# An eighth pair of every block goes through layer two in two fp32r halves, and five pairs carry 1 + ELU

## The chip, the cores and the metric

The kernel runs on one core of a Trainium2 chip. The metric is device time in microseconds (us), the median of several runs of one program. Engines: TensorE (PE, its weight loads PEld), VectorE (DVE), ScalarE (ACT), GpSimd (POOL), and SyncE (SP), which here issues DMAs.

## The reference

An induced-set attention over four batches of 12480 tokens of 128 channels, followed by a feed-forward layer of width 2048 with ELU, all in fp32:

```python
def mab(q, kv):
    s = scale * (q @ kv.transpose(0, 2, 1))
    s = s - s.max(-1, keepdims=True)
    a = np.exp(s)
    a /= a.sum(-1, keepdims=True) + 1e-09
    return a @ kv
h = mab(I, x)          # 32 inducing rows look at x
x = mab(x, h)          # x looks at the 32 rows
...
h = x @ w_in
g = np.where(h > 0.0, h, alpha * (np.exp(np.minimum(h, 0.0)) - 1.0))
return (g @ w_out).astype(np.float32)
```

## The kernel before

A batch is cut into 25 blocks, 15 of 512 tokens and 10 of 480, in seven groups of up to four. For a block the feed-forward runs over eight pairs (`cp` 0 to 7) of 128-wide slices of the hidden layer. The attention of the next batch is done beside the feed-forward of the present one; its operations are four blocks wide and small beside the pairs.

One pair in `unit`: two products of layer one put h + 1 into the PSUM tile `ph` (L980); ScalarE takes e = exp(ph - 1) (L990); VectorE takes g = min(max(ph, 1), e) (L994), which is 1 + ELU(h). What follows depends on the pair's letter:

- P: ScalarE rounds g - 1 to fp32r, `gh` (L1004); GpSimd takes 1 off g (L1020) and then writes the remainder `gl` = (g - 1) - gh (L1024).
- D: g stays in `ph`; ScalarE writes `gh` from it (L1004) and VectorE the remainder `gl` (L1010).
- N: GpSimd takes 1 off g (L1020), and the pair goes into layer two as plain fp32. M is the same with the 1 taken off on ScalarE (L1015).

Layer two (L1060) adds into one PSUM bank `po` of the block. A split pair makes six fp32r products: gh by wo_h, gh by wo_l and gl by wo_h, for two slices. A plain pair makes two fp32 products by `wo_n`. When the eighth pair is in, VectorE transposes `po` into `o` (L1075) and SP sends it off in four DMAs (L1083).

The letters are PDPDPDPN in half of the blocks and PDPDPDPM in the other half; the very first block (z) is plain in all eight pairs and reads the raw weights.

Buffers: three `ph` tiles, two `po` banks (which the small products of the attention also use), 14 rooms `sb` for e, gh and gl, and six homes `stk` that hold the attention weights of a block for layer one, filled by SP's DMAs (L947).

The order of every engine's instructions is worked out before the program is written (`Program.order`). A planner holds each operation with a cost in ns; each engine takes the operation that is ready first, and of several ready ones the one with the lowest key. The key is the number of the pair plus an offset from a table (KP, ATT, FH, KS). The order then stands fixed in the program, and each engine keeps to it.

Of the kernel before, what the change touches and what calls it, by code (L numbers as in the profile page):

```python
# [30 lines left out]
KP = {'g': 52.484375, 'px': 424.125, 'cx': -2637.046875, 'ps': 718.796875, 's': -1844.171875, 'pm': -917.6875, 'bias': -794.59375, 'exp': -1390.671875, 'eT': 883.234375, 'hh': 581.9375, 'h': -1250.90625, 'es': 527.859375, 'end': -196.765625, 'hw': 551.890625, 'win': 621.21875, 'winstep': 254.875, 'wout': -524.234375, 'woutstep': 1444.390625, 'in0': -0.359375, 'in1': 1712.046875, 'out': -245.34375, 'outstep': 241.421875, 'hwlate': 1751.796875, 'lone': -1372.359375}  # L31
# [3 lines left out]
ATT = {'first0': [996.609375, 2382.75, 1612.328125, -78.078125, 1461.875, -1378.578125, -1038.96875, -879.78125, 939.5625, 320.9375, -1571.25, -1430.9375], 'first1': [-671.8125, 1196.203125, -1397.484375, -170.328125, 176.296875, 1510.203125, 1513.703125, -312.28125, -432.71875, 1756.40625, 2562.34375, 4164.34375], 'next0': [-95.265625, -961.65625, 898.078125, 1025.671875, 539.109375, 210.140625, -860.5, 222.375, -1118.4375, -106.53125, -131.3125, 1211.5], 'next1': [-402.421875, -1166.65625, 1288.828125, 287.828125, -181.484375, 1747.34375, 341.53125, 363.625, 414.75, 243.546875, -30.828125, 634.8125], 'rest': [-67.09375, -987.203125, 716.015625, 374.046875, 595.421875, 1159.140625, 1544.3125, 273.578125, 951.0, 1170.5, 1960.46875, 164.15625]}  # L35
FH = {'xq': -451.765625, 'xT': 1142.0625, 'ps': -1349.25, 's': 1938.265625, 'pm': -448.859375, 'bias': -1055.984375, 'xm': 2688.171875, 'exp': 594.0, 'eT': 1467.703125, 'hh': -546.265625, 'h': -836.609375, 'es': 2813.640625, 'r': -1103.875, 'hn': 21.671875, 'hT': -339.75, 'hw': -606.59375}
ROOM = -39.28125
# [4 lines left out]
KINDS = {'a': 'PDPDPDPN', 'l': 'PDPDPDPN', 'z': 'NNNNNNNN', 'b': 'PDPDPDPM', 'm': 'PDPDPDPM'}  # L42
# [278 lines left out]
def kernel(  # L321
# [16 lines left out]
    for n, t in GROUPING:  # L338
# [59 lines left out]
    def new(shape, dtype, tag, name):  # L398
        return prog.tile(pools[tag], shape, dtype, tag, name)
# [20 lines left out]
    nc.gpsimd.memset(largest, 254.0)  # L420
    ind = const.tile([M, C], F32, name="ind")
    indT = const.tile([C, M], F32, name="indT")
    win_sb = const.tile([C, F], F32, name="win_sb")
    wo_n = const.tile([P, max(1, len(CHUNKS_N)), C], F32, name="wo_n")
    wo_m = const.tile([P, max(1, len(CHUNKS_M)), C], F32R, name="wo_m")
# [537 lines left out]
    def unit(b, k, cp):  # L963
# [33 lines left out]
        if how != "N":  # L997
            gh = slot(shape, F32R, f"gh_{n}", 2)
            if how == "V":
                add("DVE", n + K["gh"][cp], 0.66 * 2 * T + 60, lambda: nc.vector.tensor_scalar(  # L1000
                    out=gh(), in0=e(), scalar1=-1.0, scalar2=1.0, op0=ALU.add, op1=ALU.mult
                ), r=[(g, 0)], w=[(gh, 0)], lag=90, lock=True)
            else:
                add("ACT", n + K["gh"][cp], act(2 * T, how == "D")[0] + 20, lambda: nc.scalar.activation(  # L1004
                    gh(), ga(), AF.Copy, bias=-1.0
                ), r=[(g, 0)], w=[(gh, 0)], lag=118)
        if how in "DP":
            gl = slot(shape, F32R, f"gl_{n}", 1)
# [361 lines left out]
```

## Time and profile before

| | us |
|---|---|
| median of 3 runs (lowest, highest) | 1629.22 (1628.21, 1629.85) |
| span of the profiled execution | 1626.7 |
| PE busy | 1617.1 |
| ACT busy | 1523.5 |
| POOL busy | 1518.4 |
| DVE busy | 1487.5 |

Busy time is the union of the records of an engine. A record of a matmul ends after its last column has left the array, so consecutive records overlap; what one matmul costs a saturated TensorE is the distance from its start to the next start. An fp32 product leaves two records.

### The profile page before, as it was taken

Reading aid. Unit: us, or ns where it says so; the run is one execution under the profiler, and the core shown is the slowest. Engines: PE = TensorE matmul, PEld = TensorE weight load, DVE = VectorE, ACT = ScalarE, POOL = GpSimd, SP = SyncE. Lnnn points to the kernel's source line nnn. Section 1 sums busy time; section 2 is a strip of 40 time slices with the busy share of each in tenths; the row PEclk is TensorE's granted clock in tenths of the full one; section 3 lists DMA queues with packets and bytes.
Section 4 is the critical chain, followed back from the end, with each engine's and each line's share of the span. In section 5 each row is a group of like instructions: output and inputs, shape, how many; then the busy total and the mean of one; then the engine's idle time right before and its main releaser. Section 6 shows DMA issues by size and latency. Waiting matters only on the chain.

```text
span 1626.7 us, 23588 instructions
## 1 busy us (share of the span) xinstructions
PE 1617.1 (99%) x7820; PEld 1228.0 (75%) x7820; DVE 1487.5 (91%) x1556; ACT 1523.5 (94%) x1785; POOL 1518.4 (93%) x1018
## 2 busy tenths in 40 slices
PE   9999999999999999999999999999999999999998
PEld 7767777778777777787777777777777777777787
DVE  7799999989999999999999999999989898999997
ACT  8689999999999999999999999999999999999997
POOL 6789999999999999999999999999989999999998
PEclk9999999999999999999999999999999999999999
DMA  7442231423332133332342223322222111112111
GB/s 263 94 81 48 46 79 38 84 50 87 85 69 49 40 59 64 70 57 47 107 86 56 40 47 70 55 59 57 53 52 59 30 24 36 28 33 43 22 19 25
DMA packets 384618, 97.99 MB, mean 60 GB/s; under 512 B 364816, under 2 KB 370736, under 8 KB 384240
## 3 DMA queue, kind: packets, MB, share of 16 engines
q1 hardware_dynamic: 383504, 96.36, 27.8%
q8 instruction: 62, 1.02, 0.3%
q14 instruction: 60, 0.49, 0.1%
q10 hardware_dynamic: 992, 0.12, 0.0%
HBM read 48.94 MB, written 25.56 MB: 46 GB/s over the span
## 4 chain that ended last, share of the span: by engine, by line
PE 93%; ACT 3%; DVE 2%; issue 1%; POOL 0%; DVEq 0%; ACTq 0%; POOLq 0%
PE po L1060 65%; PE ph L980 22%; PE ps_hh L646 2%; ACT e L990 2%; ACT gh L1004 1%; PE ps_ts L803 1%; PE warm L1166 1%; PE ps_ts L558 1%; DVE e L994 1%; PE ps_s L558 1%; PE ps_x L1144 0%; PE ps_t L803 0%; DVE ph L994 0%; PE ps_warm L1109 0%; PE ps_hw L735 0%
## 5 line engine op out<-in xcount | busy, mean ns | idle before, releaser
L1024 POOL TENSOR_TENSOR gl<-e,gh 128x1024 fp32r<-128x1024 f32 (+1 forms) x396 | 931.7, 2358 | 20.0
L990 ACT ACTIVATE e<-ph 128x1024 f32<-128x1024 f32 (+1 forms) x800 | 789.9, 1010 | 58.0 <-PE ph L980 55.4
L994 DVE SCALAR_TENSOR_TENSOR e<-ph,e 128x1024 f32<-128x1024 f32 (+1 forms) x503 | 592.0, 1186 | 69.5 <-ACT e L990 63.0
L1060 PE MATMUL po<-gh,wo_h 128*128 128x512 f32 (+1 forms) x1386 | 542.4, 391 | 0.3 <-ACT gh L1004 0.3
L1060 PE MATMUL po<-gh,wo_l 128*128 128x512 f32 (+1 forms) x1386 | 536.7, 387 | 0.0
L1020 POOL TENSOR_SCALAR e<-e 128x1024 f32<-128x1024 f32 (+1 forms) x452 | 464.5, 1036 | 59.5 <-ACT gh L1004 51.3
L980 PE MATMUL ph<-stk,hw 128*128 128x512 f32 (+1 forms) x1600 | 505.7, 405 | 1.0 <-DVE e L994 0.7
L1004 ACT ACTIVATE gh<-e 128x1024 fp32r<-128x1024 f32 (+1 forms) x396 | 413.2, 1049 | 10.9 <-DVE e L994 10.2
L1060 PE MATMUL po<-gl,wo_h 128*128 128x512 f32 (+1 forms) x1386 | 416.1, 399 | 0.4 <-DVE o L1075 0.3
L994 DVE SCALAR_TENSOR_TENSOR ph<-ph,e 128x1024 f32<-128x1024 f32 (+1 forms) x297 | 354.6, 1194 | 24.1 <-ACT e L990 23.5
L980 PEld LDWEIGHTS ph<-stk,hw 128*128 128x128 f32 x1600 | 295.6, 188 | 98.6 <-issue 30.7
L1010 DVE SCALAR_TENSOR_TENSOR gl<-ph,gh 128x1024 fp32r<-128x1024 f32 (+1 forms) x297 | 351.3, 1184 | 14.9 <-ACT gh L1004 13.5
L1060 PEld LDWEIGHTS po<-gl,wo_h 128*128 128x128 f32 x1386 | 257.3, 188 | 75.2 <-issue 17.2
L1004 ACT ACTIVATE gh<-ph 128x1024 fp32r<-128x1024 f32 (+1 forms) x297 | 300.9, 1015 | 7.8 <-DVE ph L994 6.9
L1060 PEld LDWEIGHTS po<-gh,wo_h 128*128 128x128 f32 x1386 | 260.1, 188 | 60.5 <-ACT gh L1004 6.8
L1060 PEld LDWEIGHTS po<-gh,wo_l 128*128 128x128 f32 x1386 | 260.3, 188 | 53.3 <-issue 3.1
L1060 PE MATMUL po<-e,wo_n 128*128 128x512 f32 (+1 forms) x396 | 181.8, 581 | 0.0
L1060 PEld LDWEIGHTS po<-e,wo_n 128*128 128x128 f32 x396 | 74.4, 189 | 53.3 <-issue 45.4
L1075 DVE STREAM_TRANSPOSE o<-po 128x512 f32<-128x512 f32 (+1 forms) x100 | 69.1, 691 | 5.5 <-PE po L1060 4.9
L1015 ACT ACTIVATE e<-e 128x1024 f32<-128x1024 f32 (+1 forms) x51 | 53.1, 1041 | 0.1
L530 DVE STREAM_TRANSPOSE xT<-xq 128x1024 f32<-128x1024 f32 (+2 forms) x39 | 45.2, 1159 | 0.0
L935 POOL TENSOR_TENSOR alo<-aT,ahi 128x512 fp32r<-128x512 f32 (+3 forms) x28 | 35.8, 1277 | 4.3 <-ACT ahi L933 4.3
(124 smaller groups left out, 645.1 us busy)
## 6 DMA issues: line engine op xcount, KB each, us to landing
xm<-in_x_dram SPq DMA_DIRECT2D x32, 512.0 KB, 4.6
out_dram<-o SPq DMA_DIRECT2D x240, 64.0 KB, 1.9
xq<-in_x_dram SPq DMA_DIRECT2D x84, 128.0 KB, 3.0
out_dram<-o SPq DMA_DIRECT2D x158, 60.0 KB, 1.9
stk<-ahi SPq DMA_DIRECT2D x118, 64.0 KB, 2.0
xq<-in_x_dram SPq DMA_DIRECT2D x60, 120.0 KB, 2.9
stk<-ahi SPq DMA_DIRECT2D x80, 60.0 KB, 2.0
stk<-alo SPq DMA_DIRECT2D x59, 64.0 KB, 2.0
```

What stands on the lines that cost most here:

```text
L530: add("DVE", key_x, dve(n, True)[0], lambda: nc.vector.transpose(t(), xq().rearrange("p u d -> p (u d)")), r=[(xq, dq) for dq in range(4)] ...
L935: add("POOL", at(), pool_two(T)[0], lambda: nc.gpsimd.tensor_sub(alo()[:np_], aT()[:np_], ahi()[:np_].bitcast(F32)), r=[(aT, 0), (ahi, 0)] ...
L980: nc.tensor.matmul(ph()[:, j, :T], st["hw"]()[:, f * P : (f + 1) * P], homes[i][:, :T], start=True, stop=True,)
L990: add("ACT", n + K["exp"][cp], act(2 * T, True)[0] + 12, lambda: nc.scalar.activation(e(), ph()[:, :, :T], AF.Exp, bias=-1.0), r=[(ph, 0)] ...
L994: add("DVE", n + K["mid"][cp], dve(2 * T)[0] + 10, lambda: nc.vector.scalar_tensor_tensor(out=ga(), in0=ph()[:, :, :T], scalar=1.0, in1=e( ...
L1004: add("ACT", n + K["gh"][cp], act(2 * T, how == "D")[0] + 20, lambda: nc.scalar.activation(gh(), ga(), AF.Copy, bias=-1.0), r=[(g, 0)], w= ...
L1010: add("DVE", n + K["gl"][cp], dve(2 * T)[0], lambda: nc.vector.scalar_tensor_tensor(out=gl(), in0=ga(), scalar=-1.0, in1=gh().bitcast(F32) ...
L1015: add("ACT", n + K["one"][cp], act(2 * T)[0], lambda: nc.scalar.activation(e(), e(), AF.Copy, bias=-1.0), r=[(e, 0)], w=[(e, 0)], lag=118)
L1020: add("POOL", n + K["one"][cp], pool_one(2 * T)[0], lambda: nc.gpsimd.tensor_scalar(out=e(), in0=e(), scalar1=-1.0, scalar2=sign, op0=ALU. ...
L1024: add("POOL", n + K["gl"][cp], pool_two(2 * T)[0], lambda: nc.gpsimd.tensor_sub(gl(), e(), gh().bitcast(F32)), r=[(e, 0), (gh, 0)], w=[(gl ...
L1060: nc.tensor.matmul(po()[:, :T], w(), g_(), start=po.count == 0, stop=po.count == po.total - 1)
L1075: add("DVE", n + K["o"][0], dve(T, True)[0], lambda: nc.vector.transpose(o().rearrange("p u d -> p (u d)"), po()[:, :T]), r=po.parts, w=[( ...
```

## The change

All eight pairs of a block are split, in the pattern GDKDGDKG for every block but z:

- G is P without the step that takes 1 off: ScalarE rounds g itself (1 + ELU) to `gh`, GpSimd writes gl = g - gh.
- K is G with `gh` written by GpSimd instead of ScalarE.
- D stays.

Five pairs thus bring 1 + ELU into layer two, and the output carries the column sums of their ten weight slices too much. These sums are made once: ten fp32 products of a weight slice by a column of ones go into a bank `ps_sum`, and ScalarE writes them with the sign turned to `shift`. At the end of a block ScalarE copies `po` with `shift` as its bias to a new SBUF tile `ob`, and VectorE transposes `ob` instead of `po`. `wo_n` and `wo_m` go, `wo_h` and `wo_l` hold 16 slices instead of 14, there are five homes instead of six, and nearly all offsets of the planner's keys have new values. The core of the diff:

```diff
-KINDS = {'a': 'PDPDPDPN', 'l': 'PDPDPDPN', 'z': 'NNNNNNNN', 'b': 'PDPDPDPM', 'm': 'PDPDPDPM'}
+KINDS = {'a': 'GDKDGDKG', 'l': 'GDKDGDKG', 'z': 'NNNNNNNN', 'b': 'GDKDGDKG', 'm': 'GDKDGDKG'}
...
-    STK = 6
+    STK = 5
...
+            elif how == "K":
+                add("POOL", n + K["gh"][cp], pool_one(2 * T)[0], lambda: nc.gpsimd.tensor_scalar(
+                    out=gh(), in0=e(), scalar1=0.0, scalar2=1.0, op0=ALU.add, op1=ALU.mult
+                ), r=[(g, 0)], w=[(gh, 0)], lag=45)
             else:
                 add("ACT", n + K["gh"][cp], act(2 * T, how == "D")[0] + 20, lambda: nc.scalar.activation(
-                    gh(), ga(), AF.Copy, bias=-1.0
+                    gh(), ga(), AF.Copy, bias=0.0 if how == "G" else -1.0
                 ), r=[(g, 0)], w=[(gh, 0)], lag=118)
...
+        elif how in "GK":
+            pass
         elif on_act:
...
-        if how == "P":
+        if how in "PGK":
             add("POOL", n + K["gl"][cp], pool_two(2 * T)[0], lambda: nc.gpsimd.tensor_sub(
                 gl(), e(), gh().bitcast(F32)
             ), r=[(e, 0), (gh, 0)], w=[(gl, 0)], lag=50)
...
+            if raised[MIX[b][k]]:
+                ob = new([P, T], F32, "ob", f"ob_{b}_{k}")
+                add("ACT", n + K["ev"][0], act(T, True)[0], lambda: nc.scalar.activation(
+                    ob(), po()[:, :T], AF.Identity, bias=shift
+                ), r=[*po.parts, ("shift",)], w=[(ob, 0)], lag=118)
+                src, reads = (lambda: ob()), [(ob, 0)]
+            else:
+                src, reads = (lambda: po()[:, :T]), po.parts
             add("DVE", n + K["o"][0], dve(T, True)[0], lambda: nc.vector.transpose(
-                o().rearrange("p u d -> p (u d)"), po()[:, :T]
-            ), r=po.parts, w=[(o, 0)], lag=108)
+                o().rearrange("p u d -> p (u d)"), src()
+            ), r=reads, w=[(o, 0)], lag=108)
...
+    if sets:
+        chunks = sets[0]
+        ps = Bank(ps_o, "ps_sum")
+        for i, f in enumerate(chunks):
+            def column(i=i, f=f):
+                nc.tensor.matmul(ps()[:, :1], raw_out(f), ones, start=i == 0, stop=i == len(chunks) - 1)
+
+            add("PE", CH + KP["sum"] + i * KP["sumstep"], 400.0, column,
+                r=[(raws[f // (NFC // 4)], 0, "lo")], w=[(ps, 0)], lag=165)
+        add("ACT", CH + KP["sum"] + KP["sumend"], 70.0, lambda: nc.scalar.activation(
+            shift, ps()[:, :1], AF.Copy, scale=-1.0
+        ), r=[(ps, 0)], w=[("shift",)], lag=118)
```

## Rows read from the trace of the kernel before

**Rows 1.** Page: engines' busy us (share) xinstructions; granted TensorE clock in 40 slices, tenths
```profile
PE 1617.1 (99%) x7820; PEld 1228.0 (75%) x7820; DVE 1487.5 (91%) x1556; ACT 1523.5 (94%) x1785; POOL 1518.4 (93%) x1018
...
PEclk9999999999999999999999999999999999999999
```

**Rows 2.** Busy time by stretch: us; PE, PEld, DVE, ACT, POOL busy (instructions); clock, DMA
```profile
80.00:478.00 398.00, 397.26 (x1900) 297.67 (x1899) 373.20 (x386) 375.40 (x436) 369.37 (x240) 1.00 0.33 67
...
1250.00:1600.00 350.00, 349.93 (x1478) 271.10 (x1479) 318.88 (x307) 336.53 (x377) 341.35 (x215) 1.00 0.15 30
```

**Rows 3.** Waits over the span: who waited for whom, us, times, longest
```profile
ACT e L990 <- PE ph L980: 55.4, 114, 1.9
...
PEld ph L980 <- DVE e L994: 8.8, 20, 0.8
...
PEld po L1060 <- POOL gl L1024: 6.5, 24, 0.5
```

**Rows 4.** Timeline of PE, 512-token blocks: start, us, what, matmuls merged
```profile
92.64 0.63 PE L980 MATMUL ph<-stk,hw 128*128 128x512 f32 x2
93.11 1.88 PE L1060 MATMUL po<-e,wo_n 128*128 128x512 f32 x4
94.42 1.03 PE L980 MATMUL ph<-stk,hw 128*128 128x512 f32 x2
95.29 0.62 PE L1060 MATMUL po<-gl,wo_h 128*128 128x512 f32 x2
...
912.54 0.39 PE L1060 MATMUL po<-gh,wo_h 128*128 128x512 f32 x1
...
914.36 0.63 PE L980 MATMUL ph<-stk,hw 128*128 128x512 f32 x2
```

**Rows 5.** Timeline of PE, 480-token blocks at the end
```profile
1607.58 1.77 PE L1060 MATMUL po<-e,wo_n 128*128 128x480 f32 x4
...
1609.62 0.38 PE L1060 MATMUL po<-gh,wo_h 128*128 128x480 f32 x1
...
1616.57 0.38 PE L1060 MATMUL po<-gh,wo_h 128*128 128x480 f32 x1
...
1619.16 1.77 PE L1060 MATMUL po<-e,wo_n 128*128 128x480 f32 x4
```

**Rows 6.** Groups (xcount | busy us, mean ns | idle before), last row 1250 to 1600 us
```profile
L1060 PE MATMUL po<-e,wo_n 128*128 128x512 f32 x236 | 110.9, 592 | 0.0
...
L1060 PE MATMUL po<-e,wo_n 128*128 128x480 f32 x160 | 70.9, 565 | 0.0
...
L1060 PE MATMUL po<-e,wo_n 128*128 128x512 f32 (+1 forms) x92 | 42.4, 582 | 0.0
```

**Rows 7.** Page, groups of POOL and ACT: columns as in rows 6
```profile
L1024 POOL TENSOR_TENSOR gl<-e,gh 128x1024 fp32r<-128x1024 f32 (+1 forms) x396 | 931.7, 2358 | 20.0
...
L1020 POOL TENSOR_SCALAR e<-e 128x1024 f32<-128x1024 f32 (+1 forms) x452 | 464.5, 1036 | 59.5 <-ACT gh L1004 51.3
...
L1004 ACT ACTIVATE gh<-e 128x1024 fp32r<-128x1024 f32 (+1 forms) x396 | 413.2, 1049 | 10.9 <-DVE e L994 10.2
...
L1015 ACT ACTIVATE e<-e 128x1024 f32<-128x1024 f32 (+1 forms) x51 | 53.1, 1041 | 0.1
```

**Rows 8.** Groups by shape: small operations nearest to the added ones
```profile
L571 ACT COPY s<-ps_ts 128x512 f32<-128x512 f32 x9 | 5.3, 594 | 2.0 <-PE ps_ts L558 1.2 <-DVE s L901 0.8
...
L460 POOL TENSOR_SCALAR w_part<-w_part 128x512 uint32<-128x512 f32 x8 | 5.9, 732 | 4.8 <-ACT w_part L457 4.3
```

**Rows 9.** Start: small fp32 products, dummy products (`warm`), the last weights
```profile
45.44 0.28 PE L703 MATMUL ps_es<-es,sel 128*128 128x1 f32 x2
...
64.59 0.61 PE L1166 MATMUL warm<-ident 128*128 128x128 f32 x4
...
L501 POOL TENSOR_TENSOR w_out<-w_out,w_part x4: 1292/1300/1363, 12.0 to 70.6; 128x512 f32<-128x512 f32 x4
```

**Rows 10.** Table loads of ACT, and SP's waits at the homes
```profile
L866 ACT ACT_TABLE_LOAD  x1: 1283/1283/1283, 0.7 to 0.7; - x1
...
SPq L947 <- PE ph L980: 3.4, 9, 0.6
```

More of the change, by code (lines that the diff above doesn't have):

```diff
@@ L29 @@
 LOOKS = {'PE': 27.0, 'ACT': 0.0, 'DVE': 0.0, 'POOL': 0.0, 'SP': 5744.0}
-KP = {'g': 52.484375, 'px': 424.125, 'cx': -2637.046875, 'ps': 718.796875, 's': -1844.171875, 'pm': -917.6875, 'bias': -794.59375, 'exp': -1390.671875, 'eT': 883.234375, 'hh': 581.9375, 'h': -1250.90625, 'es': 527.859375, 'end': -196.765625, 'hw': 551.890625, 'win': 621.21875, 'winstep': 254.875, 'wout': -524.234375, 'woutstep': 1444.390625, 'in0': -0.359375, 'in1': 1712.046875, 'out': -245.34375, 'outstep': 241.421875, 'hwlate': 1751.796875, 'lone': -1372.359375}
+KP = {'g': 456.5, 'px': 2755.578125, 'cx': -7554.078125, 'ps': 1911.703125, 's': -5406.296875, 'pm': -3888.40625, 'bias': -2264.578125, 'exp': -8679.75, 'eT': 2665.625, 'hh': 1779.15625, 'h': -1686.546875, 'es': 424.828125, 'end': -8605.5625, 'hw': 3731.421875, 'win': 185.484375, 'winstep': 2378.4375, 'wout': 2279.15625, 'woutstep': 10260.28125, 'in0': -5247.640625, 'in1': 9487.59375, 'out': -1671.921875, 'outstep': 5346.390625, 'hwlate': 1775.671875, 'lone': -1713.921875, 'sum': 11369.375, 'sumstep': 8430.015625, 'sumend': 2638.84375}
 PHASES0 = [range(i, i + 1) for i in range(7)]
@@ L34 @@
 WALT = [1, 1, 1, 1, 1, 1, 1, 1]
-ATT = {'first0': [996.609375, 2382.75, 1612.328125, -78.078125, 1461.875, -1378.578125, -1038.96875, -879.78125, 939.5625, 320.9375, -1571.25, -1430.9375], 'first1': [-671.8125, 1196.203125, -1397.484375, -170.328125, 176.296875, 1510.203125, 1513.703125, -312.28125, -432.71875, 1756.40625, 2562.34375, 4164.34375], 'next0': [-95.265625, -961.65625, 898.078125, 1025.671875, 539.109375, 210.140625, -860.5, 222.375, -1118.4375, -106.53125, -131.3125, 1211.5], 'next1': [-402.421875, -1166.65625, 1288.828125, 287.828125, -181.484375, 1747.34375, 341.53125, 363.625, 414.75, 243.546875, -30.828125, 634.8125], 'rest': [-67.09375, -987.203125, 716.015625, 374.046875, 595.421875, 1159.140625, 1544.3125, 273.578125, 951.0, 1170.5, 1960.46875, 164.15625]}
-FH = {'xq': -451.765625, 'xT': 1142.0625, 'ps': -1349.25, 's': 1938.265625, 'pm': -448.859375, 'bias': -1055.984375, 'xm': 2688.171875, 'exp': 594.0, 'eT': 1467.703125, 'hh': -546.265625, 'h': -836.609375, 'es': 2813.640625, 'r': -1103.875, 'hn': 21.671875, 'hT': -339.75, 'hw': -606.59375}
-ROOM = -39.28125
+ATT = {'first0': [996.609375, 4248.046875, 715.546875, -6356.5625, -7769.109375, 3326.0625, 9010.21875, 235.328125, -1662.296875, -1774.96875, 1457.65625, 6895.859375], 'first1': [-7931.0625, -4302.203125, 1087.046875, 12427.78125, 4697.078125, 15310.140625, 2050.359375, 3210.703125, 567.59375, 1425.734375, 7804.125, -3108.203125], 'next0': [-95.265625, -5724.5625, 16572.09375, 3367.265625, 8425.859375, 6442.609375, 2051.578125, -3062.0, -515.9375, -8464.28125, 1821.484375, -7573.765625], 'next1': [-562.78125, -1361.359375, 8792.453125, 12922.84375, 3470.53125, 3480.21875, 8544.984375, -1119.734375, -5613.0, -801.421875, -4133.109375, -9999.328125], 'rest': [-67.046875, -8477.859375, 807.046875, -6143.25, 3194.0, 5588.265625, 9802.546875, -1317.828125, 8114.328125, 5847.234375, 4379.15625, -2462.359375]}
+FH = {'xq': -7173.953125, 'xT': 2751.984375, 'ps': -10170.921875, 's': -5113.984375, 'pm': 571.109375, 'bias': -3384.265625, 'xm': 11423.359375, 'exp': 7943.171875, 'eT': 1648.9375, 'hh': -1266.125, 'h': -6217.21875, 'es': 7219.71875, 'r': -5887.171875, 'hn': 8490.046875, 'hT': -1619.203125, 'hw': -2695.8125}
+ROOM = -1111.046875
 W4 = [1] * 8
@@ L358 @@
     NSPLIT = len(CHUNKS_S)
+    raised = {m: [f for f in range(NFC) if KINDS[m][f // 2] in "GK"] for row in MIX for m in row}
+    sets = sorted({tuple(v) for v in raised.values() if v})
+    assert len(sets) <= 1
     SCALE = 1.0 / math.sqrt(C)
     EPS = 1e-9
-    STK = 6
+    STK = 5
     bufs = dict(
-        xT=NH + 1, xq=2, xm=2, eT=2, hw=2, o=2,
+        xT=NH + 1, xq=2, xm=2, eT=2, hw=2, o=2, ob=1,
         hn=1, s2=1, aT=1, ahi=1, alo=1,
@@ L420 @@
     nc.gpsimd.memset(largest, 254.0)
+    ones = const.tile([P, 1], F32, name="ones")
+    nc.gpsimd.memset(ones, 1.0)
+    shift = const.tile([P, 1], F32, name="shift")
     ind = const.tile([M, C], F32, name="ind")
@@ L423 @@
     win_sb = const.tile([C, F], F32, name="win_sb")
-    wo_n = const.tile([P, max(1, len(CHUNKS_N)), C], F32, name="wo_n")
-    wo_m = const.tile([P, max(1, len(CHUNKS_M)), C], F32R, name="wo_m")
+    wo_n = const.tile([P, len(CHUNKS_N), C], F32, name="wo_n") if CHUNKS_N else None
+    wo_m = const.tile([P, len(CHUNKS_M), C], F32R, name="wo_m") if CHUNKS_M else None
     wo_h = const.tile([P, NSPLIT, C], F32R, name="wo_h")
@@ L1002, in unit @@
                 ), r=[(g, 0)], w=[(gh, 0)], lag=90, lock=True)
+            elif how == "K":
+                add("POOL", n + K["gh"][cp], pool_one(2 * T)[0], lambda: nc.gpsimd.tensor_scalar(
+                    out=gh(), in0=e(), scalar1=0.0, scalar2=1.0, op0=ALU.add, op1=ALU.mult
+                ), r=[(g, 0)], w=[(gh, 0)], lag=45)
             else:
                 add("ACT", n + K["gh"][cp], act(2 * T, how == "D")[0] + 20, lambda: nc.scalar.activation(
-                    gh(), ga(), AF.Copy, bias=-1.0
+                    gh(), ga(), AF.Copy, bias=0.0 if how == "G" else -1.0
                 ), r=[(g, 0)], w=[(gh, 0)], lag=118)
-        if how in "DP":
+        if how in "DPGK":
             gl = slot(shape, F32R, f"gl_{n}", 1)
```

2 lines of the change are left out of this document (1 added, 1 removed).

## The prediction

> **What bounds the kernel now.** I read the page's engine line first. PE is busy for 1617.1 us of 1626.7 and at its full clock in every slice, but ACT, POOL and DVE are at 91% to 94% too [rows 1], so the share alone doesn't tell which one sets the time. The table by stretches does: from 1250 to 1600 us PE has 349.93 us of 350 while POOL has 341.35 (97.5%) and ACT 336.53 (96.2%); in the first batch POOL and ACT have 369 and 375 of 398 us [rows 2]. The waits then say who starves whom: ACT's exp waits for layer one on PE, 55.4 us in 114 waits, and the reverse waits are small, 6.5 us of layer two for POOL's remainder and 8.8 us of layer one for VectorE to free `ph` [rows 3]. A busy PE could still be a slow PE, so the timeline has to show that it streams: eight split products go from 912.54 to 914.36, 0.228 us apart, without a hole [rows 4]. TensorE is the bound in all four batches, and POOL comes close behind it in the last.
>
> **Layer two on PE: the term that carries the sum.** In 512-token blocks the plain pair leaves four records at 93.11, two layer-one products at 94.42, and the next product starts at 95.29. That is 2.18 us; two layer-one products take 0.47 (92.64 to 93.11), so the plain pair holds PE for 1.71 us, of which 0.4 shows up only as a late start of what follows [rows 4]. A split pair is six products of 0.228 us: 1.37 us. The gain is 0.34 us. In 480-token blocks the plain pair and two layer-one products go from 1607.58 to 1609.62, 2.04 us; twelve split products take 2.59 (1616.57 to 1619.16), 0.216 each, so the plain pair is 2.04 - 0.43 = 1.61 and the split one 1.30 [rows 5]. The gain is 0.31 us. There are 236 / 4 = 59 plain pairs of the one width and 160 / 4 = 40 of the other over the span [rows 6]: 59 x 0.34 + 40 x 0.31 = 32.5 us. All of it lies on the bound, since PE has next to no idle time to put it into.
>
> The spacing of the split products is the number to distrust here: it is 0.228 us for 512 columns, where 512 columns at 2.4 GHz are 0.213 [rows 4]. The Trainium skill (TensorE: Matmul & The Clock Gate, section "Back-to-back issue gap") gives columns / 2.4 + 2.5 ns, about 0.216 and 0.203 us for the two widths. By it a split pair would be 1.29 or 1.22 us and the sum 59 x 0.42 + 40 x 0.39, an estimated 40 us. The trace disagrees, with 0.228 and 0.216 us, and decides for 32.5.
>
> **What the other engines get.** POOL: 396 remainders at 931.7 / 396 = 2.35 us become 5 x 99 = 495, plus 233 us. Of 452 steps that take 1 off, at 464.5 / 452 = 1.03 us, the eight of block z stay: minus 456. The 198 K copies are one-input instructions of the same form with an fp32r output: plus 203 at the same price [rows 7]. Net minus 20 us, to 1498. No row shows the K copy itself; the dearest one-input row of POOL takes 732 ns for 512 columns, 1.46 us for 1024 [rows 8], which would make it plus 65 instead. Nothing suggests that it gets cheaper than 1.03. I take 1.03, because L1020 is the same instruction on the same tile.
>
> ACT: 99 of the 396 `gh` from SBUF go to POOL (minus 99 x 1.04), the 51 M steps go (minus 53), and 99 copies of `po` come [rows 7]. A copy of 512 columns from PSUM is 594 ns [rows 8], and a per-partition bias may add something; between 0.55 and 0.75 us each that is plus 54 to 74. Net minus 82 to 102 us. DVE keeps eight minima, three remainders and one transpose per block, now from SBUF. Its slack of 139 us [rows 1] covers a transpose that is dearer by some tenths.
>
> So against a span of some 1597 us POOL would stand at 94%, DVE at 93%, ACT at 89%. In the stretch 1250 to 1600, 92 / 4 = 23 plain pairs fall [rows 6], so PE needs 23 x 0.325 = 7.5 us less, 342.5, and POOL, by its share of the 20 us, about 338: 98.7%, a point above now. It is the one place where POOL comes nearer to PE.
>
> **The new wait.** The block's end becomes po, ACT copy, DVE transpose, DMA. The copy waits for the last product of its block; behind it on ACT's queue stand the exps and `gh` copies of the following pairs, and for these wait VectorE's minima, and then PE through `ph` and `gh`. Behind the transpose stand minima and remainders, behind the output DMAs on SP the moves into `stk` and the loads of x. I cost it at nothing in the middle of the run, because ACT gains more slack (82 us or more) than 99 copies take. At the very end nothing covers it: the last block pays one copy and a handover, about 0.65 us. Five homes instead of six make SP wait earlier for layer one; today these waits are 3.4 us in nine times [rows 10], on a queue that PE never waits for in these rows. Nothing, at most 3 us.
>
> **The column sums.** Ten products of two records each. The nearest row, a product with one column, takes 0.28 us for two records [rows 9], so 2.8 us if all stand in PE's way, and none if they fall among the dummy products, which PE still runs at 64.59; the last weights are ready only at 70.6 + 1.3 us [rows 9], and four of the ten products need those. I take 1.2. They also hold one of the two `po` banks meanwhile, in a stretch where block z alone needs one.
>
> **The order.** All keys are new, so the order on every engine is; no row shows it. Idle time on PE could fall by at most the 15 us of the reverse waits named above, or grow. I take nothing, because the stretch from 1250 to 1600 shows that this planner holds PE full with two other engines above 96%.
>
> **Sum.** 1626.7 - 32.5 + 0.65 + 1.2 = 1596 us of span. The median of the runs lies 2.5 us above this span, so the prediction is 1599 us, 1.9% less.
>
> **Rivals.**
> - POOL becomes the bound. For it: 98.7% in the last batch, and K and G put every fp32r remainder but D's on POOL. If no engine here gets beyond the 97.5% that POOL shows, the last batch is 338 / 0.975 = 347 instead of 342.5, and the kernel ends at 1603. If the K copy costs 1.46 us, POOL has 1583 us, and at 97.5% the span is 1624, the time 1626: no change. Against: POOL's total falls, and L1020 gives the price. Chance 0.14 for some of the gain lost this way (1606 to 1626), 0.04 for all of it.
> - The ACT copy stalls ACT's queue, and the kernel gets slower. Each late last product holds up the exps behind the copy, and layer one on PE runs dry with only three `ph` tiles. An ACT wait for PE is 55.4 / 114 = 0.49 us on average [rows 3]. If each of 99 copies passes that on to PE, 48 us come on top: 1648. It decides from 32 / 99 = 0.33 us per block on. Against: ACT gains slack, and there are two `po` banks. Chance 0.10.
> - The copy isn't free of tables. The trace has one table load, 1.28 us, for exp, relu and copies [rows 10], and the changed function (Identity with a bias) is not in it. Two loads per block would be 2 x 99 x 1.28 = 254 us on ACT, 1524 - 95 + 254 = 1683 busy: some 1710 us. Chance 0.01. The Trainium skill (ScalarE: Activation LUTs, section "Table sets: the hidden batching unit") says that copy and identity are in every set, by which no load would come; no row here shows Identity.
> - More than forecast: with ACT freed, exps come sooner and the 15 us of reverse waits shrink by half or more. 1585 to 1592. Chance 0.11.
>
> **How the numbers follow.** The likeliest case, 1592 to 1606, has 0.60. A difference under 0.2% (3.3 us) can't be told from no change. Faster holds the forecast, the larger gain and the part-way case: 0.84. The same: 0.05, the dear K copy and its neighbours. Slower: 0.11, the queue stall and the tables. The range from 1591 to 1624 leaves out the upper end of the slower cases and most of the larger gain.
>
> **What the changed profile would show.** No plain pairs but z's 32 records; 1584 records each of gh by wo_h, gh by wo_l and gl by wo_h, still 0.228 and 0.216 us apart; POOL with 495 remainders, 198 copies near 1.03 us, and busy near 1498; ACT near 1430 with 99 copies of 0.55 to 0.75 us and one table load; PE near 99% of a shorter span. The prediction is wrong if PE shows waits for ACT or POOL of more than some 30 us, if POOL's copies are near 1.5 us, or if the first 80 us grow by more than the sums.

## The result and the profile after

The changed kernel takes **1605.55 us** (1605.26 to 1607.94), the kernel before 1628.86 in the same comparison (1628.21 to 1629.85). The ratio is 0.986, 95% interval 0.9846 to 0.9874: 23.3 us or 1.4% faster. Predicted were 1599 us in a range from 1591 to 1624.

The profiled execution of after is the slowest of its four, 1607.94 us with a span of 1605.8; the spans of the others are 1603.1 to 1603.6. Its mean granted clock is 0.997, that of the others 0.999; the stretch where it fell, 30 to 40 us, is shown in the last section.

The page, first the engines' busy time and the granted clock (answers to [rows 1]):

```profile
PE 1593.2 (99%) x8038; PEld 1270.8 (79%) x8038; DVE 1488.3 (93%) x1556; ACT 1449.7 (90%) x1734; POOL 1499.1 (93%) x871
...
PEclk9999999999999999999999999999999999999999
```

Busy time by stretch, columns and stretches as in [rows 2]:

```profile
80.00:478.00 398.00, 397.14 (x1983) 314.41 (x1982) 380.07 (x392) 363.16 (x431) 371.40 (x207) 1.00 0.35 70
...
1250.00:1600.00 350.00, 349.31 (x1551) 285.69 (x1549) 319.47 (x304) 322.09 (x367) 340.75 (x181) 1.00 0.15 29
```

PE is still the engine without a gap, 397.14 of 398 and 349.31 of 350 us; POOL has 340.75 of 350 in the last batch, 97.4%, where the prediction feared 98.7%. The waits (who for whom, us, times, longest; answers to [rows 3]):

```profile
ACT e L996 <- PE ph L986: 91.3, 184, 1.6
...
PEld po L1072 <- POOL gl L1036: 7.5, 22, 0.9
PEld ph L986 <- DVE e L1000: 5.7, 14, 0.8
...
ACT ob L1089 <- PE po L1072: 5.9, 10, 1.6
```

ScalarE waits for layer one more often than before (184 times, 114 before) and PE waits hardly more for POOL (7.5 us, 6.5 before): PE starves the others, not they PE. The new wait, ScalarE's copy for the block's last product, is 5.9 us in ten of 99 blocks. One wait grew that the prediction took for small, SP's at the homes for layer one, from 3.4 us in nine times (beside [rows 10]):

```profile
SPq L953 <- PE ph L986: 147.5, 31, 14.1
```

No wait of PE for these DMAs shows, so it lies beside the chain. The groups of the changed steps (answers to [rows 7, 10]):

```profile
L1036 POOL TENSOR_TENSOR gl<-e,gh 128x1024 fp32r<-128x1024 f32 (+1 forms) x495 | 1157.1, 2359 | 29.5 <-ACT gh L1014 16.3 <-POOL gl L1036 1.0
...
L1010 POOL TENSOR_SCALAR gh<-e 128x1024 fp32r<-128x1024 f32 (+1 forms) x198 | 204.5, 1033 | 36.8 <-DVE e L1000 32.3 <-PE ph L986 3.5 <-POOL gl L1036 0.3
...
L872 ACT ACT_TABLE_LOAD x1 | 1.3, 1283 | 0.7 <-PEq L1384 0.7
```

ScalarE's copies by shape (beside [rows 8]):

```profile
L1089 ACT ACTIVATE ob<-po,shift 128x512 f32<-128x512 f32 x59 | 41.3, 700 | 2.5 <-PE po L1072 2.5
...
L1089 ACT ACTIVATE ob<-po,shift 128x480 f32<-128x480 f32 x40 | 26.9, 673 | 3.4 <-PE po L1072 3.4
```

495 remainders, 198 copies at 1.03 us on POOL, 99 copies on ScalarE and one table load: the change does what it says. POOL's durations are those that the prediction took, and the copy lies inside its bounds.

**Where the time went.** PE's timeline gives the price of a product. In a 512-token stretch of after, 46 products of layers one and two start from 912.36 to 923.01; in a 480-token stretch 32 start from 1591.69 to 1598.64 (start, us, what, matmuls merged):

```profile
912.36 0.39 PE L1072 MATMUL po<-gh,wo_h 128*128 128x512 f32 x1
...
923.01 0.40 PE L1072 MATMUL po<-gh,wo_h 128*128 128x512 f32 x1
...
1591.69 0.38 PE L1072 MATMUL po<-gh,wo_h 128*128 128x480 f32 x1
...
1598.64 0.38 PE L1072 MATMUL po<-gh,wo_h 128*128 128x480 f32 x1
```

That is 10.65 / 46 = 0.2315 us and 6.95 / 32 = 0.2172 us a product. In before, 52 products of 512 columns start from 917.47 to 929.47, 0.2308 us each:

```profile
917.47 0.63 PE L980 MATMUL ph<-stk,hw 128*128 128x512 f32 x2
...
929.47 0.40 PE L1060 MATMUL po<-gh,wo_h 128*128 128x512 f32 x1
```

With the two prices of after, and a plain pair at 1.71 and 1.61 us as in the prediction (over 95 of the 99 plain pairs of before the same reading gives 1.72 and 1.61 on average), all start-to-start distances of PE's records between the first output and the last product divide like this:

| us | before | after |
|---|---|---|
| layers one and two, products at these prices | 1457.7 | 1428.1 |
| attention's small products, column sums | 68.1 | 67.7 |
| left over: holes and late starts | 15.9 | 19.1 |
| first output to last product | 1541.7 | 1514.9 |

A late start is a product that begins after its turn although PE shows no hole. The first output's transpose starts at 79.96 us before and 85.33 after (VectorE's timelines, first before, then after), and from the start of the last product to the end it is 4.88 and 5.49 us:

```profile
79.96 0.71 DVE L1075 STREAM_TRANSPOSE o<-po 128x512 f32<-128x512 f32 x1
```

```profile
85.33 0.69 DVE L1095 STREAM_TRANSPOSE o<-po 128x512 f32<-128x512 f32 x1
```

So -26.8 in the middle, +5.4 at the start and +0.6 at the end make the 20.9 us between the two spans, to 0.1 us. The profiled execution of after is 2.4 us longer than the median. Four kernels below that keep its order, at a granted clock of 0.999, have their first output at 81.6 to 82.8 us instead of 85.3, so I put these 2.4 us down to the start; the executions of after that were not profiled don't show it. Without them the gain is the 23.3 us of the medians.

### The profile page after: what moved, and what is told of

The parts are those of the page before. It is cut to its first block, busy times and chain, and to the rows that moved or that the text cites. A ratio compares the mean times of both kernels' runs of the same rounds, so it can differ in the third digit from the quotient of the medians.

```text
span 1605.8 us, 23962 instructions
## 1 busy us (share of the span) xinstructions
PE 1593.2 (99%) x8038; PEld 1270.8 (79%) x8038; DVE 1488.3 (93%) x1556; ACT 1449.7 (90%) x1734; POOL 1499.1 (93%) x871
## 4 chain that ended last, share of the span: by engine, by line
PE 90%; DVE 2%; ACT 2%; DMA 2%; POOL 2%; issue 1%; SPq 0%; POOLq 0%; DVEq 0%; ACTq 0%
PE po L1072 63%; PE ph L986 21%; PE ps_hh L652 2%; POOL gl L1036 1%; DMA w_out<-in_moe_w_out_dram 1%; PE ps_ts L809 1%; PE ps_ts L564 1%; ACT e L996 1%; PE warm L1186 1%; DVE e L1000 1%; ACT gh L1014 1%; DMA xm<-in_x_dram 1%; DVE gl L1020 0%; POOL gh L1010 0%; PE ps_s L564 0%
## 5 line engine op out<-in xcount | busy, mean ns | idle before, releaser
L1036 POOL TENSOR_TENSOR gl<-e,gh 128x1024 fp32r<-128x1024 f32 (+1 forms) x495 | 1157.1, 2359 | 29.5 <-ACT gh L1014 16.3
L996 ACT ACTIVATE e<-ph 128x1024 f32<-128x1024 f32 (+1 forms) x800 | 790.3, 1011 | 95.6 <-PE ph L986 91.3
L1072 PE MATMUL po<-gh,wo_h 128*128 128x512 f32 (+1 forms) x1584 | 615.5, 389 | 0.3 <-ACT ob L1089 0.3
L1072 PE MATMUL po<-gh,wo_l 128*128 128x512 f32 (+1 forms) x1584 | 614.4, 388 | 0.0
L1072 PE MATMUL po<-gl,wo_h 128*128 128x512 f32 (+1 forms) x1584 | 456.2, 390 | 2.2 <-POOL gl L1036 1.0
L1072 PEld LDWEIGHTS po<-gh,wo_h 128*128 128x128 f32 x1584 | 297.4, 188 | 65.8 <-ACT gh L1014 3.2
L1072 PEld LDWEIGHTS po<-gh,wo_l 128*128 128x128 f32 x1584 | 297.9, 188 | 57.1
L1014 ACT ACTIVATE gh<-e 128x1024 fp32r<-128x1024 f32 (+1 forms) x297 | 309.0, 1043 | 10.2 <-DVE e L1000 6.1
L1010 POOL TENSOR_SCALAR gh<-e 128x1024 fp32r<-128x1024 f32 (+1 forms) x198 | 204.5, 1033 | 36.8 <-DVE e L1000 32.3
L1089 ACT ACTIVATE ob<-po,shift 128x512 f32<-128x512 f32 (+1 forms) x99 | 68.2, 689 | 5.9 <-PE po L1072 5.9
L1095 DVE STREAM_TRANSPOSE o<-ob 128x512 f32<-128x512 f32 (+1 forms) x99 | 67.9, 686 | 4.5 <-ACT ob L1089 4.4
```

The source lines that it names most:

```text
L996: add("ACT", n + K["exp"][cp], act(2 * T, True)[0] + 12, lambda: nc.scalar.activation(e(), ph()[:, :, :T], AF.Exp, bias=-1.0), r=[(ph, 0)] ...
L1010: add("POOL", n + K["gh"][cp], pool_one(2 * T)[0], lambda: nc.gpsimd.tensor_scalar(out=gh(), in0=e(), scalar1=0.0, scalar2=1.0, op0=ALU.ad ...
L1072: nc.tensor.matmul(po()[:, :T], w(), g_(), start=po.count == 0, stop=po.count == po.total - 1)
L1089: add("ACT", n + K["ev"][0], act(T, True)[0], lambda: nc.scalar.activation(ob(), po()[:, :T], AF.Identity, bias=shift), r=[*po.parts, ("sh ...
L1095: add("DVE", n + K["o"][0], dve(T, True)[0], lambda: nc.vector.transpose(o().rearrange("p u d -> p (u d)"), src()), r=reads, w=[(o, 0)], l ...
```

## The experiments

Twelve kernels ran, each beside the kernel before on the same chip (1628.4 to 1628.9 us). Of these, three were re-planned by the kernel's own planner without my meaning it; they tell of the order and nothing else.

**plain_pe: the product term alone.** Order and all other engines as after; pair 7 goes through PE as two fp32 products, as pair 7 did before.

```diff
+            plain = cp == 7 and MIX[b][k] != "z"
...
-                for _, w, g_ in piece:
+                for _, w, g_ in piece if not plain else () if m else piece[::2]:
...
-                        po()[:, :T], w(), g_(), start=po.count == 0, stop=po.count == po.total - 1
+                        po()[:, :T], w().bitcast(F32) if plain else w(), g_().bitcast(F32) if plain else g_(),
```

> The changed kernel, in the same order, but PE's share of the eighth pair as before the change: two fp32 products instead of six fp32r ones (its remainder is not used; all other engines do what they did). Theory: PE gets 59 x 0.32 + 40 x 0.30 = 31 us more, and the time rises by 29 to 33 us to 1635 to 1638.5. Rival (the gain came from ScalarE's smaller load): the rise is under 10 us.

Measured: 1640.63 us (1639.62 to 1641.59), 35.1 more than after; ratio to before 1.0075 (1.006 to 1.009). The stretch from first output to last product is 1550.4 us, 35.5 more. The time is 2 us above the upper end of what I expected: by the prices above the products make 31.3 us of it, and the other 4 are holes and late starts. So the split of the eighth pair is worth the whole gain and more, by PE alone: without it, the change with all its relief for ScalarE is slower than the kernel before. The rival, that the gain comes from ScalarE's smaller load, falls: that load is as small here (1451.7 us busy). Layer one's products stand 0.251 us apart here in 512-token blocks, 0.238 after: the late start behind a fp32 product, which the prediction counted into the pair's 1.71 us, shows there.

**less_pe: how far below PE is the next bound?** The two gl products of pair 7 go; everything else keeps its order.

```diff
+            drop = m == 1 and cp == 7 and MIX[b][k] != "z"
...
-                for _, w, g_ in piece:
+                for _, w, g_ in () if drop else piece:
```

> The changed kernel, in the same order, without the two gl products of the eighth pair (198 of 4752 left out; the output lacks them). Theory: PE is the bound, 198 x 0.226 = 45 us less PE work, and POOL is the next bound at 1499 us: at the share it reached, 97.5%, the last batch stands at 350 us and gains nothing, the other batches gain 34 us: 1568 to 1575. Rival (POOL is the bound already): 1600 or more.

Measured: 1591.95 us (1591.77 to 1593.01), ratio 0.9777 (0.9763 to 0.9792): 13.6 us less where 45 us of PE's work went. Theory and rival both missed: PE is the bound, but in this order only by some 14 us. The page's line of this kernel, its waits, and the shares of its chain:

```profile
PE 1568.3 (99%) x7840; PEld 1216.6 (77%) x7840; DVE 1484.3 (93%) x1556; ACT 1448.1 (91%) x1734; POOL 1498.6 (94%) x871
```

```profile
PEld po L1073 <- POOL gl L1036: 25.4, 62, 0.9
PEld ph L986 <- DVE e L1000: 15.8, 46, 0.8
PEld ph L986 <- DVE gl L1020: 12.9, 38, 1.1
```

```profile
PE 53%; POOL 17%; DVE 11%; ACT 9%; issue 6%; DMA 3%; SPq 0%; POOLq 0%; DVEq 0%; ACTq 0%
```

The waits that PE's weight loads hardly had in after (7.5 us for POOL, 5.7 and 1.8 for VectorE) are 25.4 and 28.7 us here, and PE's share of the chain falls from 90% to 53%. By the prices above 44.7 us of products go and 30 us of holes and late starts come. No engine beside PE is above 94%; POOL and VectorE, and to a lesser degree ScalarE, take over together in this fixed order. A new plan for it was not tried. PE's line says 99% all the same: modelled ends of matmuls cover the short holes.

**less_pool: is POOL's 93% already a bound?**

```diff
+            def remainder():
+                if cp == 6:
+                    nc.gpsimd.tensor_sub(gl()[:, :, :32], e()[:, :, :32], gh()[:, :, :32].bitcast(F32))
+                else:
+                    nc.gpsimd.tensor_sub(gl(), e(), gh().bitcast(F32))
...
-                    parts.append((2, lambda f=f: wo_h[:, WHERE_S[f], :], lambda j=j: gl()[:, j]))
+                    parts.append((2, lambda f=f: wo_h[:, WHERE_S[f], :], lambda j=j: gl()[:, j] if cp != 6 else wo_l.rearrange("p c d -> p (c d)")[:, :T]))
```

> As the kernel after, in the same order, but GpSimd's remainder for pair 6 (which carries 1 + ELU) is made for 32 columns of each slice instead of all, and the two products of that pair that read it take a constant tile instead: part of the computation is left out. 99 instructions of 2.36 us shrink to about 0.15 us each, some 218 us of GpSimd's 1499 us, while TensorE has as many products as before. Theory: TensorE's products set the end and GpSimd's 93% lies beside them, so only what PE waits for that remainder goes (7.5 us of such waits in the profile of after, spread over all eight pairs, so about 1 us for one of them, and up to some 5 us with those that follow from them): 1600 to 1605 us. Rival, that GpSimd at 93% is a bound next to PE: a seventh less of its work would give 1590 us or less.

Measured: 1603.27 us (1602.58 to 1606.64), ratio 0.9846 (0.9833 to 0.986). As the theory said, and 2.3 us under after; the fastest and slowest runs of the two overlap. The page's line of this kernel, and its waits:

```profile
PE 1588.6 (99%) x8038; PEld 1269.6 (79%) x8038; DVE 1488.1 (93%) x1556; ACT 1448.9 (90%) x1734; POOL 1304.1 (81%) x871
```

```profile
PEld po L1077 <- ACT gh L1014: 4.3, 15, 0.8
...
PEld po L1077 <- POOL gl L1040: 1.4, 3, 0.8
```

195 us less on POOL (218 were estimated) take the wait of PE's weight loads for it from 7.5 to 1.4 us; their wait for ScalarE's `gh` goes from 3.2 to 4.3 us. With PE at its full work POOL alone is no bound.

**pool_more: what carrying 1 + ELU is for.** One more pass on GpSimd in each G pair.

```diff
+            def remainder():
+                if how == "G":
+                    nc.gpsimd.tensor_scalar(
+                        out=e(), in0=e(), scalar1=0.0, scalar2=1.0, op0=ALU.add, op1=ALU.mult
+                    )
+                nc.gpsimd.tensor_sub(gl(), e(), gh().bitcast(F32))
```

> As the kernel after, in the same order, but GpSimd makes one more pass over the activation in each of the three pairs that don't carry 1 + ELU (in place, times one plus zero; 297 more instructions of about 1.03 us, 306 us), which is GpSimd's load if all eight pairs were split and each formed ELU on GpSimd. Theory, that carrying 1 + ELU is what makes room for the eighth split pair: GpSimd becomes the bound at (1499 + 306) / 0.97 to 0.98 or so, 1840 to 1860 us. Rival, that GpSimd's extra work lies in its idle time and beside PE as most else does: it has 107 us of idle time, so the least is 1605 + 306 - 107 = 1804 us if the bound is GpSimd at 100%; anything under 1790 us would say that GpSimd's busy time is overstated by the profile.

Measured: 1880.71 us (1879.75 to 1881.71), ratio 1.1546 (1.1531 to 1.1562). The page's line of this kernel, and its waits:

```profile
PE 1672.5 (89%) x8038; PEld 1252.6 (67%) x8038; DVE 1512.5 (81%) x1556; ACT 1471.1 (78%) x1734; POOL 1798.1 (96%) x1168
```

```profile
PEld po L1078 <- POOL gl L1041: 267.1, 240, 2.5
...
PE po L1078 <- POOL gl L1041: 166.6, 190, 2.1
```

299 us more on POOL cost 275 us. PE drops to 89%. Its weight loads wait 267 us for the remainder and its products 167 us; these are in large part the same waits and don't add, as PE has no more than 206 us outside its busy time. That is the load of eight split pairs with every ELU formed on GpSimd, in an order not made for it; POOL's 1798 us are more than the whole time before, so no other order would bring that kernel under it. Taking the 1 off on another engine was not tried. With GpSimd the two halves of the change belong together: the split takes PE's time away, the carried 1 makes room on POOL. The time came out 20 to 40 us above what I expected: POOL reaches 96% in this order, not 97 to 98.

**no_copy_kept: ScalarE's copy.** The copy is left out and VectorE transposes `po` at the copy's place in the order.

```diff
-                add("ACT", n + K["ev"][0], act(T, True)[0], lambda: nc.scalar.activation(
-                    ob(), po()[:, :T], AF.Identity, bias=shift
+                add("ACT", n + K["ev"][0], act(T, True)[0], lambda: nc.vector.transpose(
+                    o().rearrange("p u d -> p (u d)"), po()[:, :T]
...
-            add("DVE", n + K["o"][0], dve(T, True)[0], lambda: nc.vector.transpose(
+            add("DVE", n + K["o"][0], dve(T, True)[0], lambda: None if raised[MIX[b][k]] else nc.vector.transpose(
```

> As the kernel after, with every engine's order the same except that ScalarE's copy of the output (99 of 700 and 673 ns, 68.2 us) is left out and VectorE transposes straight from the accumulator at the place in the order where the copy stood; the column sums are not taken off, so that part of the computation is left out. Theory: the copy lies beside TensorE's work, apart from the tail (about 0.65 us) and the bank of the accumulator that comes free earlier: 1603 to 1605 us, 0.5 to 2 us under the kernel after. Rival, that the copy in ScalarE's queue holds up the ELU behind it and costs part of the gain (ScalarE's waits for layer one grew from 55 to 91 us): 1600 us or less.

Measured: 1619.71 us (1619.07 to 1622.41), ratio 0.9946 (0.9934 to 0.9959): 14 us *slower* than after. Theory and rival both missed. Its waits (columns as above):

```profile
ACT e L996 <- PE ph L986: 126.1, 235, 1.8
...
ACT gh L1014 <- DVE ph L1000: 23.5, 41, 2.6
...
PE po L1072 <- DVE o L1089: 4.8, 9, 1.1
```

ScalarE waits 23.5 us for VectorE's minima (7.1 after), and PE waits 4.8 us for the transposes to give the bank free. The edit moves VectorE's transposes forward as well as taking the copy out, so the 14 us are the price of the two together. That the copy alone is no burden is likely from its own waits in after (5.9 us on ScalarE, at most 2.6 us on PE for `ob`), but no run takes it out by itself. What the run does show is that 46 us less on ScalarE (1403.2 against 1449.7 busy) buy nothing when VectorE has to transpose at the copy's place.

**no_sums: the column sums.** Order kept, the ten products and the step to `shift` left out, `shift` zero.

```diff
+    nc.gpsimd.memset(shift, 0.0)
...
-                nc.tensor.matmul(ps()[:, :1], raw_out(f), ones, start=i == 0, stop=i == len(chunks) - 1)
+                pass
```

> The changed kernel, in the same order, without the ten column products; shift is filled with zeros, so the column sums are not taken off. Theory: eight records ran among dummy products and twelve cost some 1.1 us on PE, so the time falls by 0.5 to 1.5 us. Rival (sums delay the start): it falls by 4 us or more.

Measured: 1605.32 us (1604.76 to 1606.71), ratio 0.9856 (0.9841 to 0.9871): 0.2 us, nothing, where 0.5 to 1.5 were expected. The group of the sums in after (columns as in [rows 6]):

```profile
L1266 PE MATMUL ps_sum<-ones,w_out 128*128 128x1 f32 x20 | 2.6, 239 | 0.0
```

These 2.6 us of records lie between 53.9 and 102.0 us, eight of the twenty among dummy products and twelve among those of the first two blocks. The start of this kernel is as late as any with this order (first output 82.6 us): the sums don't delay it.

**start_keys and load_keys: the start.** The keys of the start from the kernel before (`KP`, with the three new ones of the sums), and then only those eight that place the loads and weight steps, were meant to give the old start back.

```diff
-KP = {'g': 456.5, 'px': 2755.578125, ...
+KP = {'g': 52.484375, 'px': 424.125, ...
```

> The changed kernel with the start's key offsets (table KP) of the kernel before; only the three offsets of the column sums stay new. Theory: the start is late because VectorE stands behind a weight step that waits 13 us for w_out, so PE idles at 30 us and the first product of block z into po begins at 65.8 us instead of 60.0. With the old offsets it begins near 60 to 61 and the time falls by 3 to 6 us, to 1600 to 1602.5. Rival (the column sums and the bank that they hold make the start late): the first product stays near 65 and the time within 1.5 us of 1605.5.

> The changed kernel with only the offsets of the weight loads and weight steps (in0, in1, out, outstep, win, winstep, wout, woutstep) of the kernel before. If the order of loads and weight steps alone is the cause, this gives back as much as all start offsets: 3 to 6 us, PE no longer idle near 30 us. If it is the order of the attention's own steps in the start, the time stays within 1.5 us of 1605.5.

Measured: 1700.94 us (1700.14 to 1703.69), ratio 1.0445 (1.0429 to 1.046), and 1701.0 us (1699.79 to 1705.21), ratio 1.0447 (1.0431 to 1.0462). A clean miss, by 100 us. The start did not come back, it came later still: the first output is at 116.17 us in start_keys and 112.6 in load_keys, 85.33 in after (a row of VectorE's timeline in start_keys).

```profile
116.17 0.70 DVE L1095 STREAM_TRANSPOSE o<-po 128x512 f32<-128x512 f32 x1
```

Busy time by stretch in start_keys (columns as in [rows 2]), and one of its waits:

```profile
478.00:871.00 393.00, 371.46 (x1744) 285.40 (x1744) 345.49 (x350) 329.87 (x388) 339.63 (x187) 0.97 0.29 59
...
1250.00:1600.00 350.00, 348.77 (x1603) 279.38 (x1602) 324.38 (x320) 321.49 (x371) 339.21 (x184) 1.00 0.18 38
```

```profile
PEld po L1072 <- POOL gl L1036: 19.8, 55, 1.3
```

A few keys of the start change the planner's choices for batches 0 to 2 as well: from some 330 to 500 us, and again in the batches behind, outputs leave in pairs, some 30 us and then 2 us apart, where after has 7 to 27; PE falls to 371.46 of 393 us and its granted clock to 0.97. The last 2222 records of PE are in the order of after and take as long as there, 474 us: PE is full again. The work is the same to the instruction. The order alone is worth four times the change.

**no_copy: a third one re-planned.** The transpose was to read `po` directly, with the copy's step emptied.

```diff
-                add("ACT", n + K["ev"][0], act(T, True)[0], lambda: nc.scalar.activation(
-                    ob(), po()[:, :T], AF.Identity, bias=shift
-                ), r=[*po.parts, ("shift",)], w=[(ob, 0)], lag=118)
-                src, reads = (lambda: ob()), [(ob, 0)]
+                add("ACT", n + K["ev"][0], act(T, True)[0], lambda: None, r=[*po.parts, ("shift",)], w=[(ob, 0)], lag=118)
+                src, reads = (lambda: po()[:, :T]), [(ob, 0), *po.parts]
```

> The changed kernel, in the same order, without the ScalarE copy at the end of a block: VectorE transposes po itself, and the column sums are not taken off. Theory: the 99 copies (68 us on ACT) lie beside PE's work, only the last one shows: minus 0.6 to 1.5 us. Rival (a copy that waits for PE holds up the exps): minus 5 us or more, and ACT's waits for layer one fall from 91 us.

Measured: 1753.6 us (1752.45 to 1756.3), ratio 1.0769. The planner saw the bank held longer and made another order, with outputs in pairs again, so this run does not tell of the copy.

**late_w_out and late_all: the weights' steps in the start.** In the profile of after, VectorE and ScalarE both stand for 3.2 us at the load of a quarter of the second layer's weights (the load itself is 13 us under way), the small step `bias` stands behind them, and PE has a hole (start, us, what, idle before it and its releaser):

```profile
30.60 0.43 DVE L456 TENSOR_SCALAR w_part<-w_out 128x512 uint32<-128x512 uint32 x1 [3.17 <-DMA w_out<-in_moe_w_out_dram]
30.94 0.17 DVE L607 TENSOR_REDUCE bias<-ps_pm 128x1 f32<-128x16 f32 x1
...
31.16 1.93 PE L652 MATMUL ps_hh<-xm,eT 128*32 128x128 f32 x32 [1.57 <-DVE bias L607]
```

The first kernel sorts this quarter's steps 3 us later on every engine, the second most steps of the two quarters after it by 4 us too; all else keeps its place.

```diff
+    late = lambda quarter, step: 3000.0 * (quarter == 5)
...
+        at_ = o.start + late(*getattr(o, "step", (0, 0)))
+        then[o] = max([at_] + [then[p] + 0.01 for p in o.before])
+    todo.sort(key=lambda o: then[o])
```

> The changed kernel with every step of the second w_out quarter moved 3 us later in each engine's order; everything else keeps its order. Theory: VectorE and ScalarE no longer stand 3.2 us behind a transfer that lands at 30.6 us, PE doesn't idle there and keeps its full clock, the first product of block z into po begins at 62 to 64 us instead of 65.8, and the time falls by 1.5 to 4 us, to 1601.5 to 1604. Rival (the new start is late for other reasons): within 1 us of 1605.5.

> As the one before, and the later steps of the third and fourth quarter of w_out 4 us later as well, so that VectorE's long steps at 51 and 55.5 us leave the chain to block z. Theory: another 1 to 2 us gained, 1600 to 1603; it costs what it gains if block z then waits for its weights (its first po product early, its last one late).

Measured: 1608.31 us (1607.37 to 1608.35), ratio 0.9875 (0.986 to 0.989), and 1612.44 us (1612.1 to 1612.8), ratio 0.9902 (0.9886 to 0.9919). Both are slower than after, where 1.5 to 5.5 us less were expected. The hole at 30 us is gone in both, but the first output comes at 84.5 and 88.5 us. In late_w_out PE now waits for the first layer's weights, in late_all the first block's products wait for a step on GpSimd that stands behind weight steps in its queue (rows of PE's timelines, first late_w_out, then late_all):

```profile
54.23 0.62 PE L748 MATMUL ps_hw<-win_sb,hT 128*32 128x512 f32 x1 [0.92 <-POOL win_sb L514]
```

```profile
71.02 1.99 PE L1079 MATMUL po<-e,w_out 128*128 128x512 f32 x4 [1.89 <-POOL e L1039]
```

The middle is nearly unchanged (1514.9 and 1515.9 us). So the hole alone does not set the first output: the steps of the weights set it as soon as they come later.

**early_w_out: the load instead of the steps.** The load in question is issued ahead of the last two loads of x.

```diff
+    loads = [o for o in todo if o.eng == "SP"]
+    first = next(o for o in loads if o.key == -1988.0)
+    quarter = loads[loads.index(first) + 2]
+    todo.remove(quarter)
+    todo.insert(todo.index(first), quarter)
```

> As the kernel after, with one difference: the load of the weights of layer two's second quarter is issued ahead of the last two loads of the input's rows (491 KB) instead of behind them, all engines' orders kept. VectorE and ScalarE waited 1.6 us (3.2 in the profile of after) for that load at 31 us, and the weights' steps behind it are on the way to the first output. Theory, that the landing of this load delays the start: 1.0 to 1.5 us less, 1603.5 to 1605 us. Rival, that the weights' steps themselves (VectorE's, stretched beside GpSimd's) or the rows now landing later set the first output: 1605 to 1607 us, no change or slower.

Measured: 1604.42 us (1603.54 to 1604.58), ratio 0.9849 (0.9836 to 0.9862). All four executions lie under the fastest of after (1605.26), though the intervals of the two ratios overlap: 1.1 us, as the theory said, and the fastest kernel here that does the whole computation. PE has no hole at 30 us any more (30.56 against 31.16; a row of its PE timeline), and the first output comes at 81.8 us:

```profile
30.56 1.08 PE L652 MATMUL ps_hh<-xm,eT 128*32 128x128 f32 x32
```

## Why the prediction was right, step by step

- **What bounds the kernel: right.** plain_pe and less_pool show it from both sides, more work for PE costs its full price and less work for POOL gives 2.3 us, hardly more than the runs of one kernel differ by. What the prediction did not see is how near the next bound lies: in this order 14 us by less_pe. It called POOL "close behind" only for the last batch.
- **Layer two on PE, -32.5: right in kind, a little too large.** I took 0.228 us from one run of eight products; over 46 products of after it is 0.2315, over 52 of before 0.2308, and 0.2172 for 480 columns. So the spacing did not grow with the change; the eight products were a fast stretch. A split pair thus costs 1.39 and 1.30 us, and the term is 59 x 0.32 + 40 x 0.31 = 31.3 us. The rule of the Trainium skill (TensorE: Matmul & The Clock Gate, section "Back-to-back issue gap"), which would have given 40 us, is off further still: 0.216 and 0.203 us by it, 0.2315 and 0.2172 measured. That section of the Trainium skill gives this formula for an isolated matmul; its figure for a stream with weight loads, about 131 ns at 512 columns, is further off yet for these fp32r products.
- **The order, 0: the step that was mis-sized in the middle.** Holes and late starts are 19.1 us against 15.9, so the new order gives 3.2 us back. That it is so little is the merit of these very keys; the three re-planned kernels are 95 to 148 us slower than after. "I take nothing" held for this program, but the reason I gave, that the planner holds PE full, was no reason: the same planner did not in start_keys.
- **The start, +1.2 for the sums: wrong cause.** The sums cost 0.2 us (no_sums). The start is nevertheless 1.6 to 3.7 us later in the profiles of the six kernels that keep this order (first output 81.6 to 82.8 us in plain_pe, pool_more, less_pe, no_sums and less_pool, 83.7 in no_copy_kept; 79.96 before), and before has by then done seven more products, 1.6 us. So the start costs some 3 to 5 us; that 1.2 of them stood in the sum was luck. The prediction named a start that grows by more than the sums as a sign against it, and so it was. About 1 us of it is the late load (early_w_out). late_w_out and late_all show that later weight steps make the start later, so the rest may hang on that chain; that was not shown, nor which step of it.
- **The tail, +0.65: right**, 0.6.
- **POOL, 1498: right**, 1499.1, with the copy at 1033 ns. The dear copy of 1.46 us did not come. For the last batch the prediction's 338 us should be 337 by its own share of the 20 us, 98.4% instead of 98.7%; that changes nothing in the sum.
- **ScalarE, near 1430: 20 us too low.** The copies (68.2 us) lie inside the bounds. By the union of its records, the `gh` copies give 93 us back and the M steps 47, the copies take 57, and the same 800 exps take 8 more, though a single one takes the same time (1010 and 1011 ns): more of them start after a wait and overlap less with the record before. It lies beside PE's work.
- **The copy's wait, 0 in the middle: right.** 5.9 us in all for ScalarE, and PE waits at most 2.6 us for `ob`. The rival of a stalled queue at 1648 did not come. What the time would be with the copy alone left out stays open. SP's waits at the five homes grew far more than the prediction's words suggest, to 147.5 us, but they cost PE nothing, as it said.
- **The table rival:** one load, as before. The trace agrees with the Trainium skill (ScalarE: Activation LUTs, section "Table sets: the hidden batching unit") for Identity.

So the gain is 23.3 us where the sum had 30.6, and the time 6.5 us above the forecast: 1.2 us come from the product's spacing, 3.2 from the order, and the rest, some 3, from the start.

## What to carry to other kernels

- Price a streamed product by the mean distance over many of them in the running kernel, and test a gain on one engine by putting its work alone back (plain_pe): that separates it from all the relief that comes with it.
- Ask how far below the bound the next one lies, with a kernel that takes more from the bound than you mean to (less_pe). Here 45 us less on PE were worth 14 us with the order held; waits for POOL and VectorE took the rest.
- Where a planner fixes the order, a changed key, read or cost re-draws the whole program, and the new order can cost more than the change gives; an experiment is only one if the order is held.

## What the runs showed of the hardware

- fp32r products with new weights each, 128 x 512 and 128 x 480, stream at 0.2315 and 0.2172 us on average; single runs go as low as 0.228 and 0.216.
- ScalarE's copy of 512 columns from PSUM with a bias per partition (Identity, after) took 700 ns, the plain copy without one (before) 594 ns [rows 8].
- After PE's hole of 1.57 us at 31 us the granted clock of the stretch 30 to 40 us is 0.66: it spends part of it at 1.2 GHz, the lower level, and the 32 small products behind the hole take 1.93 us. In early_w_out, without the hole, the same stretch has 1.00 and the same products take 1.08 us. First after, then early_w_out (columns as in [rows 2]):

```profile
30.00:40.00 10.00, 8.84 (x117) 5.80 (x117) 7.42 (x19) 8.12 (x17) 2.40 (x8) 0.66 0.34 112
```

```profile
30.00:40.00 10.00, 10.00 (x156) 7.98 (x157) 9.44 (x25) 10.00 (x23) 4.26 (x12) 1.00 0.44 147
```

A hole does not always do this. less_pool and no_copy_kept have two holes each at the same places, of 0.65 and 0.57 us and of 0.65 and 0.59 us, at 30 and 32 us; the granted clock stays at 1.00 in the first and is 0.83 in the second. First less_pool, then no_copy_kept:

```profile
30.00:40.00 10.00, 8.88 (x139) 6.47 (x140) 9.11 (x24) 10.00 (x22) 3.20 (x11) 1.00 0.33 107
```

```profile
30.00:40.00 10.00, 9.33 (x131) 6.34 (x132) 8.28 (x22) 9.01 (x20) 2.42 (x8) 0.83 0.25 79
```
